# Taking 1/sum out of a DMA transpose and v out of a casting DMA, in a thresholded-attention and MLP kernel

## The chip, the cores and the metric

The kernel runs on one core of a Trainium2 chip, as one program from start to end. The metric is the device time of one execution in microseconds (us). A core has five engines with a queue each, worked off in order: PE (TensorE, matmuls; its weight loads are listed as PEld), DVE (VectorE), ACT (ScalarE), POOL (GpSimd) and SP (SyncE, which here only issues DMAs). They wait for each other through semaphores. PE writes to PSUM alone, eight banks of 2 KB in each of 128 partitions; ACT and DVE read PSUM; POOL works in SBUF.

## The reference

There are 8 batches, 8 heads, 576 tokens and 64 channels per head. After attention, the heads of a token are laid side by side (512 channels) and go through two linear layers.

```python
scores = scale * q @ k.T                        # per batch and head, 576 x 576
thresh = max(scores, -1) - tau                  # tau = 0.02
scores = where(scores >= thresh, scores, -1e9)
attn = exp(scores - max(scores, -1))
attn = attn / (sum(attn, -1) + 1e-9)
x = (attn @ v)                                  # tokens x 512 when the heads are joined
h = x @ w_in                                    # 512 -> 2048
out = maximum(0.01 * h, h) @ w_out              # 2048 -> 512
```

## The kernel before

The attention is cut into 72 **periods**, nine in each batch: for each half of the first 512 tokens (256 queries) four periods, one per pair of heads, and a ninth, the tail period, for the last 64 tokens of all heads. One period is four score tiles of 128 x 576: two query tiles `c` by two heads `h` of a pair. Period n of the main loop makes, in this order:

- PE: the scores (L223, 24 matmuls, each product as three fp16 halves); the turn of a q or k pair that a later period needs (L169, 16 small transposes into two PSUM banks, `tp`); then, in two halves, second-layer units (L369, two at a time, 8 matmuls), a first-layer unit (L356, 16 matmuls), again both; last the product of weights and v (L316, `pv`) of the period n - 2 (`PV_LAG`).
- DVE: four copies of score tiles out of PSUM, which also take the row minima (L256); 1/sum of the period before (L295) after the first copy; DVE's part of the turn's copy (L181, bank 1); the threshold (L267); three of the four weight tiles with their sums (L289); between the second and the third of these, `pv` times 1/sum into `x` (L336, in tail periods L328).
- ACT: its part of the turn's copy (L181 or L178, bank 0), the exponential of three tiles (L278), the leaky ReLU of each first-layer unit out of PSUM (`g`, L358), in every second period the copy of a finished 128 x 512 output (`osb`, L375), and the fourth tile's weights in two steps (L283, L284).
- POOL: splits one q or k pair into fp16 halves (L133, L140, L144) behind DVE's last weight tile of the period before, so that it runs beside the copies out of PSUM; between L133 and L140 it widens 1/sum to 64 columns per head as **a tenth block of the weights** (L299); it issues the loads of v and of the MLP's weights as DMAs that cast fp32 to fp16 (L92, L99, L103, L106).
- SP: turns the weights of the period before with one DMA transpose (L304: ten blocks of 128 for each c, fp16), then issues the period's loads of q and k, then stores.

PSUM has one tag `h` with two banks. A turn takes both, and then first-layer outputs `hp`, `pv` and the next turn take them in rotation, so the first `hp` of a period gets the bank that ACT's turn copy has emptied. In the first six periods (`early`), `pv` stands in front of the MLP's units, and 12 dummy matmul pairs (L481) fill PE in the first five. The order on each engine is the order in which the loop writes it; there is no scheduler.

Of the kernel before, what the change touches and what calls it, by code (L numbers as in the profile page):

```python
# [36 lines left out]
def kernel(  # L37
# [30 lines left out]

    raws, tails = {}, {}
    SRC = {"q": q, "k": k}  # L70
# [25 lines left out]
    def load_vtails(b):  # L96
        src = v[b, :, MAIN:S, :].rearrange("(r h) p d -> h p r d", h=2)
        for h in range(2):
            nc.gpsimd.dma_start(out=v16[b % 2][ds(64 * h, 64), :, 4 + h, :], in_=src[h])  # L99

# [21 lines left out]
    def new_half():  # L122
        return sb.tile([128, 2, 4, 2, 64], FP16, tag="half", bufs=6, name="half")

# [33 lines left out]
    def turn(keys, tags=("h", "h")):  # L158

        n = 2 if keys[0][1] == "t" else 4  # L160
        tp = [ps.tile([128, len(keys), 2, n, 64], FP16, tag=tag, bufs=2 if tag == "h" else 1, name="tp")
              for tag in tags]
        for i, key in enumerate(keys):
            half = halves.pop(key)
            for x in range(2):
                for t in range(n):
                    for r in range(2):
                        rows = ds(64 * r, 64)
                        nc.tensor.transpose(tp[r][:, i, x, t, :], half[rows, x, t, :, :].rearrange("p h d -> p (h d)"),  # L169
                                            ident[rows, rows])  # L170
            tps[key] = [t[:, i, :, :, :] for t in tp]

    def take(key, r, copy):
# [119 lines left out]
    def recip(st):  # L293
        rec = sb.tile([128, 2, 2], FP32, tag="rec", bufs=2, name="rec")
        nc.vector.reciprocal(out=rec[:, :, :], in_=st.sum[:, :, :])  # L295
        st.rec = rec

    def widen(st):
        nc.gpsimd.tensor_copy(out=st.w[:, :, 9, :].rearrange("q c (h d) -> q c h d", h=2),  # L299
                              in_=st.rec[:, :, :].unsqueeze(3).to_broadcast([128, 2, 2, 64]))  # L300

    def turn_w(st):
        st.wt = sb.tile([128, 2, 10, 128], FP16, tag="wT", bufs=4, name="wT")
        nc.sync.dma_start_transpose(out=st.wt[:, :, :, :].rearrange("k c n q -> k (c n) q"),  # L304
                                    in_=st.w[:, :, :, :].rearrange("q c n d -> q (c n d)"))

    def pv(st):
# [13 lines left out]
    def evacuate(st, ready):  # L321
        if st.tail:
            if st.b % 2 == 0:
                groups["t"] = xg = Group(128, (st.b, None))
                xg.x = sb.tile([128, NP, 128], FP16, tag="xt", bufs=2, name="xt")
            xg = groups["t"]
            o = xg.x[:, :, ds(64 * (st.b % 2), 64)]
            nc.vector.tensor_tensor(out=o, in0=st.pv[:, :, :].rearrange("d c (u q) -> d (c u) q", u=2),  # L328
                                    in1=st.wt[:, :, 9, :].rearrange("d c (u q) -> d c u q", u=2), op=AX.mult)
            done = st.b % 2 == 1  # L330
        else:
            if st.p == 0:
                groups["m"] = xg = Group(256, (st.b, 2 * st.blk))
                xg.x = sb.tile([128, NP, 256], FP16, tag="x", bufs=3, name="x")
            xg = groups["m"]
            nc.vector.tensor_tensor(out=xg.x[:, st.p, :].rearrange("d (c q) -> d c q", c=2), in0=st.pv[:, :, :],  # L336
                                    in1=st.wt[:, :, 9, :], op=AX.mult)
# [51 lines left out]

    loads_at, turns_at, split_at_, issue_at = {}, {}, {}, {}  # L390

    def at(d, n, f):
        d.setdefault(n, []).append(f)

    def split_pool(key, behind=None, between=lambda: None):
# [3 lines left out]
        between()  # L399
        split_high(key)  # L400
        split_low(key)
# [15 lines left out]
    for p in (2, 3):  # L417
        load_pair(p, "k", nc.sync)
        load_pair(p, "q", nc.sync)
    load_tails(0, "q")  # L420
    for t in v16:
# [18 lines left out]
    for i in range(4):  # L440
        load_w(i)
    for h in range(2):
        load_v(0, h)
    load_vtails(0)
    for key in ((0, 1, "k"), (0, 1, "q")):
# [8 lines left out]
    for key in ((0, 3, "k"), (0, 3, "q")):  # L454
        at(turns_at, 2, key)
    at(turns_at, 3, (0, "t", "q"))
    for i in range(4):
        at(issue_at, 5 + i, lambda i=i: load_w(4 + i))

    for b in range(1, B):  # L460
        base = PERB * (b - 1)
        for i, (s, w_) in enumerate(((0, "k"), (0, "q"), (1, "k"), (1, "q"))):
            at(loads_at, base + ((0, 1, 5, 6)[i] if b > 1 else (1, 2, 5, 6)[i]),
               lambda b=b, s=s, w_=w_: load_main(b, s, w_))
        for w_ in "kq":
            at(loads_at, base + (2 if b > 1 else 3), lambda b=b, w_=w_: load_tails(b, w_))
        order = [(0, "k"), (0, "q"), ("t", "k"), ("t", "q"), (1, "k"), (1, "q"), (2, "k"), (2, "q"), (3, "k"), (3, "q")]
        slots = (3, 4, 5, 5, 6, 7, 8, 9, 10, 11) if b > 1 else (4, 5, 7, 7, 6, 8, 9, 10, 11, 11)
        for n, (p, w_) in zip(slots, order):
            split_at(base + n, (b, p, w_))  # L470
        for h in range(2):
# [11 lines left out]

    def pv_of(n, ready):
        if n >= PV_LAG and n - PV_LAG < N:
            pv(periods[n - PV_LAG])
            return lambda: evacuate(periods[n - PV_LAG], ready)
        return lambda: None

    N = len(periods)  # L490
    n = 0
    while n < N + PV_LAG or l1q or l2q or stores:
        st = periods[n] if n < N else None
        before = periods[n - 1] if 1 <= n <= N else None
        early = n < 6
        keys = turns_at.get(n, [])
# [3 lines left out]
        if st:  # L500
            scores(st)
        if first_:
            turn(first_)
        if st:
# [4 lines left out]
        for i, key in enumerate(todo):  # L509
            if i == 0 and n > 2:  # L510
                split_pool(key, before.last, lambda: widen(before))
            else:
                split_pool(key)
# [12 lines left out]
        for f in issue_at.get(n, []):  # L526
            f()
        if st:
            exp_plain(st, 0)
        if early:  # L530
            if n < 5:
                idle(6)
            pv_of(n, n)()
            if n < 5:
                idle(6)
        for half in range(2):
            for _ in range(2):
                if l2q:
                    layer2()
            if l1q and l1q[0][3] <= n:  # L540
                layer1()
            if half == 0:
                for key in second:
                    turn([key])
            if st:
                if half == 0:
                    exp_plain(st, 1)
                    exp_plain(st, 2)
                    for key in second:
                        take(key, 0, on_act)  # L550
                else:
                    exp_steep(st, 3)
        x = (lambda: None) if early else pv_of(n, n + 1)
        if st:
# [3 lines left out]
        if st:  # L558
            weights(st, 1)
        x()  # L560
        if st:
# [35 lines left out]
```

## Time and profile before

| | |
|---|---|
| median of 3 runs | 522.95 us (522.0 to 527.2) |
| profiled execution | 523.43 us, of which the span is 521.6 us |
| PE, DVE, ACT, POOL busy | 88%, 85%, 77%, 44% of the span |
| DMA transposes of weights | 72, median 6.5 us from issue to landing |
| v loads through POOL | 16 of 256 KB (median 7.3 us), 16 of 32 KB (5.0 us) |

An entry such as `L256 DVE ... s<-sc` names the line of the kernel, the engine, and which tile is made from which. Times of single instructions overlap a little, since an engine starts one while the last of the former drains; the distance from start to start is what an engine can keep up. An idle time is put down to whatever ended last before the waiting instruction. "PEclk" is the clock that PE was granted, as a share of the full one.

### The profile page before, as it was taken

What the parts mean: (1) busy time and instruction counts of PE and PEld (TensorE: products, weight loads), DVE (VectorE), ACT (ScalarE), POOL (GpSimd) and SP (SyncE); (2) the same over time, 40 slices, a digit from 0 to 9 for tenths busy, and PEclk for the clock granted to TensorE, in tenths of its full rate; (3) what the DMA queues carried; (4) which work ended last, traced back from release to release, by engine and by line L of the source; (5) the groups of instructions that cost most, each with busy time, mean ns of one, the idle gap of its engine ahead of it and who ended that gap; (6) DMA issues with size and microseconds to landing.
All of it is one profiled execution on the core that took longest, in us unless ns stands there. A gap on an engine that the chain in (4) does not pass through costs nothing. (4 is left out here: it accounts for less than half of the span.)

```text
span 521.6 us, 19185 instructions
## 1 busy us (share of the span) xinstructions
PE 460.3 (88%) x7864; PEld 364.2 (70%) x7864; DVE 443.2 (85%) x1314; ACT 400.3 (77%) x704; POOL 228.2 (44%) x357
## 2 busy tenths in 40 slices
PE   3477674987989999989999999989999989999995
PEld 2455653665878777867788787877787868777773
DVE  3969693989999999999999999999999999999200
ACT  4737482778999988887879898879889987888541
POOL 5924372535554545454544555445545454000000
PEclk9969796999999999999999999999999999999999
DMA  8987999969989999989978999999998998656511
GB/s 211 178 183 125 159 170 142 202 122 169 192 160 201 146 213 166 183 165 174 205 154 192 139 223 165 201 149 209 153 212 160 178 176 167 133 103 153 133 43 60
DMA packets 230808, 85.65 MB, mean 164 GB/s; under 512 B 201024, under 2 KB 227648, under 8 KB 230720
## 3 DMA queue, kind: packets, MB, share of 16 engines
q1 hardware_dynamic: 214416, 75.12, 74.5%
q0 software_dynamic: 15488, 8.92, 14.0%
q8 instruction: 61, 1.00, 0.8%
q10 hardware_dynamic: 816, 0.39, 0.3%
q14 instruction: 27, 0.22, 0.1%
HBM read 36.70 MB, written 9.44 MB: 88 GB/s over the span
## 5 line engine op out<-in xcount | busy, mean ns | idle before, releaser
L256 DVE TENSOR_SCALAR_CACHE_REDUCE s<-sc 128x576 f32<-128x576 f32 x288 | 208.7, 745 | 5.2 <-PE sc L223 4.2
L289 DVE SCALAR_TENSOR_TENSOR w<-s,th,e 128x576 f16<-128x576 f32 x216 | 176.0, 840 | 9.0 <-ACT e L278 1.9
L278 ACT ACTIVATE e<-s,mn 128x576 f16<-128x576 f32 x216 | 158.7, 769 | 12.2 <-DVE s L256 12.0
L356 PEld LDWEIGHTS <-win 128*64 128x64 f16 x2560 | 134.5, 111 | 32.6 <-issue 9.3
L369 PE MATMUL o<-wout,g 128*64 128x512 f16 x1152 | 150.3, 383 | 0.7 <-ACT osb L375 0.7
L356 PE MATMUL hp<-x,win 128*64 128x256 f16 x2048 | 135.8, 275 | 5.9 <-ACT qT L181 2.6
L223 PE MATMUL sc<-kT,qT 64*128 64x384 f16 (+7 forms) x1920 | 124.3, 292 | 8.7 <-DVE qT L181 6.8
L358 ACT ACTIVATE g<-hp 128x512 f16<-128x512 f32 x144 | 85.4, 593 | 45.4 <-PE hp L356 44.2
L223 PEld LDWEIGHTS <-qT 64*128 64x128 f16 (+1 forms) x1920 | 94.3, 99 | 31.2 <-issue 13.0
L133 POOL TENSOR_SCALAR scaled<-raw 128x512 f32<-128x512 f32 x60 | 37.6, 627 | 161.7 <-DVE w L289 114.8
L369 PEld LDWEIGHTS <-g 128*64 128x64 f16 x1152 | 62.0, 110 | 35.3 <-issue 3.5
L144 POOL TENSOR_TENSOR half<-scaled,half 128x512 f16<-128x512 f32 (+1 forms) x75 | 80.9, 1079 | 6.4
L316 PE MATMUL pv<-wT,v 128*64 128x256 f16 (+1 forms) x960 | 54.5, 252 | 28.8 <-DMA wT<-w 28.8
L316 PEld LDWEIGHTS <-v 128*64 128x64 f16 x960 | 41.2, 112 | 33.7 <-DMA wT<-w 29.7
L284 ACT ACTIVATE w<-s,minus_tau 128x576 f16<-128x576 f32 x72 | 55.8, 775 | 6.0 <-issue 0.4
L283 ACT ACTIVATE s<-s,th 128x576 f32<-128x576 f32 x72 | 55.7, 773 | 0.8 <-DVE th L267 0.7
L299 POOL CAST w<-rec 128x256 f16<-128x256 f32 x72 | 29.2, 405 | 57.6 <-DVE rec L295 53.1
L169 PE MATMUL tp<-ident,half 64*128 64x64 f16 x1152 | 33.4, 194 | 12.5 <-ACT half L154 6.8
L140 POOL CAST half<-scaled 128x512 f16<-128x512 f32 (+1 forms) x75 | 43.5, 580 | 0.8
L169 PEld LDWEIGHTS <-half 64*128 64x128 f16 x1152 | 30.2, 97 | 19.1 <-issue 9.6
L336 DVE TENSOR_TENSOR x<-pv,wT 128x256 f16<-128x256 f32 x64 | 26.9, 421 | 19.3 <-PE pv L316 19.2
L181 ACT COPY kT<-tp 128x512 f16<-128x512 f16 x32 | 18.6, 580 | 21.8 <-PE tp L169 21.3
(39 smaller groups left out, 248.5 us busy)
## 6 DMA issues: line engine op xcount, KB each, us to landing
out_dram<-osb SPq DMA_DIRECT2D x16, 512.0 KB, 6.0
raw<-in_k_dram SPq DMA_DIRECT2D x14, 512.0 KB, 4.9
raw<-in_q_dram SPq DMA_DIRECT2D x14, 512.0 KB, 5.1
v<-in_v_dram POOLq DMA_DIRECT2D x16, 256.0 KB, 7.3
win<-in_moe_w_in_dram POOLq DMA_DIRECT2D x4, 512.0 KB, 8.5
wout<-in_moe_w_out_dram POOLq DMA_DIRECT2D x4, 512.0 KB, 11.4
wT<-w SPq DMA_TRANSPOSE x72, 6.5
raw<-in_k_dram SPq DMA_DIRECT2D x4, 256.0 KB, 5.9
```

The costliest lines, as they stand in the source:

```text
L144: nc.gpsimd.tensor_tensor(out=halves[key][:, 1, 0:n, :, :], in0=scaled.pop(key)[:, 0:n, :, :], in1=halves[key][:, 0, 0:n, :, :], op=AX.sub ...
L169: nc.tensor.transpose(tp[r][:, i, x, t, :], half[rows, x, t, :, :].rearrange("p h d -> p (h d)"), ident[rows, rows])
L223: yield nc.tensor.matmul(out=o, lhsT=lhs, rhs=turned[st.b, "k"][rows, kx, pair, ds(key0, n)], start=(i == 0), stop=(i == 2), skip_group_ch ...
L256: return nc.vector.tensor_scalar(out=st.s[TILES[n]][:, :], in0=sc[:, ds(PLACE[TILES[n]], 576)], scalar1=-1.0 / UNIT, scalar2=None, op0=AX. ...
L278: nc.scalar.activation(out=st.e[t][:, :], in_=st.s[t][:, :], func=AF.Exp, bias=st.mn[:, n : n + 1], scale=-1.0)
L283: nc.scalar.activation(out=z, in_=z, func=AF.Prelu, bias=st.th[:, n : n + 1], scale=-1.0, alpha=1e20)
L284: nc.scalar.activation(out=w_of(st, t), in_=z, func=AF.Exp, bias=minus_tau[:, :], scale=1.0, accum_out=st.sum[:, c, h : h + 1])
L289: st.last = nc.vector.scalar_tensor_tensor(out=w_of(st, t), in0=st.s[t][:, :], scalar=st.th[:, n : n + 1], in1=st.e[t][:, :], op0=AX.is_le ...
L316: nc.tensor.matmul(out=o, lhsT=v16[st.b % 2][:, 2 * c + u if st.tail else st.p, blk, :], rhs=rhs, start=(i == 0), stop=(i == 4), skip_grou ...
L356: nc.tensor.matmul(out=hp[ds(64 * c, 64), jj, :], lhsT=w_in16[:, i, ds(128 * j + 64 * c, 64)], rhs=g.x[:, i, :], start=(i == 0), stop=(i = ...
L358: nc.scalar.activation(out=g.g[:, ds(nj * u, nj), :], in_=hp[:, :, :], func=AF.Prelu, bias=0.0, scale=1.0, alpha=0.01)
L369: nc.tensor.matmul(out=g.o[ds(64 * c, 64), :], lhsT=g.g[:, j, ds(128 * m + 64 * c, 64)], rhs=w_out16[:, j, :], start=(j == 0), stop=(j == ...
```

## The change

1/sum is no longer part of the tile that the DMA turns: `w` and `wT` have nine blocks for each c instead of ten, and the widening on POOL goes. DVE writes 1/sum as fp16. PE spreads and turns it: four transposes for the period n - 2 (two query tiles, two heads; a column of 1/sum, read 64 times over, against the identity), right behind the scores and the first turn of period n, into the unused upper half of the bank that the turn takes first; without a turn it takes a bank of tag `h` of its own. ACT copies the 128 x 256 result out (`by`) behind its turn copies, and DVE's product reads `by`.

v is loaded as fp32 by SP, four heads at a time (512 KB, two loads in a batch, and two for the tail), into staging tiles, and cast to fp16 by POOL: two copies of 128 x 256 per pair of heads, at the end of POOL's work in four of nine periods, the tail's two copies in the last of these; batch 0's first pair and tail by ACT in period 0. One of six staging tiles for halves goes. For the periods 2 to 4, `pv` moves from the front to the end of the period, as in the later ones; the dummy matmuls stand in one run.

```diff
-        st.w = sb.tile([128, 2, 10, 128], FP16, tag="w", bufs=3, name="w")
+        st.w = sb.tile([128, 2, 9, 128], FP16, tag="w", bufs=3, name="w")
...
     def recip(st):
-        rec = sb.tile([128, 2, 2], FP32, tag="rec", bufs=2, name="rec")
-        nc.vector.reciprocal(out=rec[:, :, :], in_=st.sum[:, :, :])
-        st.rec = rec
-
-    def widen(st):
-        nc.gpsimd.tensor_copy(out=st.w[:, :, 9, :].rearrange("q c (h d) -> q c h d", h=2),
-                              in_=st.rec[:, :, :].unsqueeze(3).to_broadcast([128, 2, 2, 64]))
+        st.rec = sb.tile([128, 2, 2], FP16, tag="rec", bufs=4, name="rec")
+        with nc.allow_low_precision(reason="as the weights"):
+            nc.vector.reciprocal(out=st.rec[:, :, :], in_=st.sum[:, :, :])
...
+    def spread(st, bank):
+        bank = bank or ps.tile([128, 1024], FP16, tag="h", bufs=2, name="tp")
+        for c in range(2):
+            for h in range(2):
+                nc.tensor.transpose(bank[ds(64 * h, 64), ds(512 + 128 * c, 128)],
+                                    st.rec[:, c, ds(h, 1)].to_broadcast([128, 64]), ident[:, :])
+        return bank
+
+    def take_spread(st, bank):
+        st.by = sb.tile([128, 2, 128], FP16, tag="by", bufs=2, name="by")
+        nc.scalar.copy(out=st.by[:, :, :], in_=bank[:, 512:768].rearrange("d (c q) -> d c q", c=2))
...
-    def load_v(b, h):
-        nc.gpsimd.dma_start(
-            out=v16[b % 2][:, :, ds(6 * h, 4), :].rearrange("p r t d -> p r (t d)"),
-            in_=v[b, :, 0:MAIN, :].rearrange("(r h) (p t) d -> h p r (t d)", h=2, t=4)[h])
+    def load_v(b, s):
+        t = sb.tile([128, 4, 256], FP32, tag="vraw", bufs=2, name="vraw")
+        nc.sync.dma_start(out=t[:, :, :], in_=v[b, ds(4 * s, 4), 0:MAIN, :].rearrange("h (p t) d -> p h (t d)", t=4))
+        vraws[b, s] = t
...
+    def cast_v(b, p, copy=None):
+        copy = copy or nc.gpsimd.tensor_copy
+        src = vraws[b, p // 2][:, ds(2 * (p % 2), 2), :].rearrange("p h (t d) -> p h t d", d=64)
+        dst = v16[b % 2][:, p, :, :].rearrange("p (h t) d -> p h t d", h=2)
+        for h in range(2):
+            copy(out=dst[:, h, ds(h, 4), :], in_=src[:, h, :, :])
...
-        if first_:
-            turn(first_)
+        bank = turn(first_) if first_ else None
+        due = periods[n - PV_LAG] if PV_LAG <= n < N + PV_LAG else None
+        if due:
+            bank = spread(due, bank)
...
         if before:
-            if not todo or n <= 2:
-                widen(before)
             turn_w(before)
+        for f in pool_at.get(n, []):
+            f()
...
+        if due:
+            take_spread(due, bank)
         if st:
             exp_plain(st, 0)
...
-        for h in range(2):
-            at(issue_at, base + 4 + 3 * h, lambda b=b, h=h: load_v(b, h))
-        at(issue_at, base + 8, lambda b=b: load_vtails(b))
+        for s in range(2):
+            at(loads_at, base + 4 + 3 * s, lambda b=b, s=s: load_v(b, s))
+        at(loads_at, base + 8, lambda b=b: load_vtails(b))
+        for p in range(NP):
+            at(pool_at, base + (6, 7, 9, 10)[p], lambda b=b, p=p: cast_v(b, p))
+        at(pool_at, base + 10, lambda b=b: cast_vtails(b))
```

More of the change, by code (lines that the diff above doesn't have):

```diff
@@ L89, in load_tails, with cast_vtails @@
         tails[b, which] = t
-    def load_v(b, h):
-        nc.gpsimd.dma_start(
-            out=v16[b % 2][:, :, ds(6 * h, 4), :].rearrange("p r t d -> p r (t d)"),
-            in_=v[b, :, 0:MAIN, :].rearrange("(r h) (p t) d -> h p r (t d)", h=2, t=4)[h])
+    def load_v(b, s):
+        t = sb.tile([128, 4, 256], FP32, tag="vraw", bufs=2, name="vraw")
+        nc.sync.dma_start(out=t[:, :, :], in_=v[b, ds(4 * s, 4), 0:MAIN, :].rearrange("h (p t) d -> p h (t d)", t=4))
+        vraws[b, s] = t
     def load_vtails(b):
+        t = sb.tile([128, NP, 64], FP32, tag="vrawt", bufs=1, name="vrawt")
         src = v[b, :, MAIN:S, :].rearrange("(r h) p d -> h p r d", h=2)
         for h in range(2):
-            nc.gpsimd.dma_start(out=v16[b % 2][ds(64 * h, 64), :, 4 + h, :], in_=src[h])
+            nc.sync.dma_start(out=t[ds(64 * h, 64), :, :], in_=src[h])
+        vtails[b] = t
+    def cast_v(b, p, copy=None):
[4 more added lines that the diff above has]
+            copy(out=dst[:, h, ds(h, 4), :], in_=src[:, h, :, :])
+    def cast_vtails(b, copy=None):
+        copy = copy or nc.gpsimd.tensor_copy
+        t = vtails.pop(b)
+        for h in range(2):
+            copy(out=v16[b % 2][ds(64 * h, 64), :, 4 + h, :], in_=t[ds(64 * h, 64), :, :])
     def load_w(i):
@@ L122, in new_half @@
     def new_half():
-        return sb.tile([128, 2, 4, 2, 64], FP16, tag="half", bufs=6, name="half")
+        return sb.tile([128, 2, 4, 2, 64], FP16, tag="half", bufs=5, name="half")
     def split_scale(key):
@@ L160, in turn @@
         n = 2 if keys[0][1] == "t" else 4
-        tp = [ps.tile([128, len(keys), 2, n, 64], FP16, tag=tag, bufs=2 if tag == "h" else 1, name="tp")
-              for tag in tags]
+        banks = [ps.tile([128, 1024], FP16, tag=tag, bufs=2 if tag == "h" else 1, name="tp") for tag in tags]
+        tp = [t[:, 0 : 128 * n * len(keys)].rearrange("d (i x t p) -> d i x t p", x=2, t=n, p=64) for t in banks]
         for i, key in enumerate(keys):
@@ L171, in turn @@
             tps[key] = [t[:, i, :, :, :] for t in tp]
+        return banks[0]
     def take(key, r, copy):
@@ L387, in store, with split_pool @@
                 nc.sync.dma_start(out=out[ds((b + u) * S + MAIN, 64), :], in_=g.osb[ds(64 * u, 64), 0, :])
-    loads_at, turns_at, split_at_, issue_at = {}, {}, {}, {}
+    loads_at, turns_at, split_at_, pool_at, act_at = {}, {}, {}, {}, {}
     def at(d, n, f):
         d.setdefault(n, []).append(f)
-    def split_pool(key, behind=None, between=lambda: None):
+    def split_pool(key, behind=None):
         mm = split_scale(key)
@@ L398, in split_pool @@
             tc.add_manual_dep(mm.ins, behind.ins.name, BEHIND, reason="beside VectorE's reads of PSUM")
-        between()
         split_high(key)
@@ L419 @@
         load_pair(p, "q", nc.sync)
+    for s in range(2):
+        load_v(0, s)
+        if s == 0:
+            load_vtails(0)
     load_tails(0, "q")
@@ L456 @@
     at(turns_at, 3, (0, "t", "q"))
+    at(act_at, 0, lambda: cast_v(0, 0, on_act))
+    at(act_at, 0, lambda: cast_vtails(0, on_act))
+    for p in range(1, NP):
+        at(pool_at, 2, lambda p=p: cast_v(0, p))
     for i in range(4):
-        at(issue_at, 5 + i, lambda i=i: load_w(4 + i))
+        at(pool_at, 5 + i, lambda i=i: load_w(4 + i))
     for b in range(1, B):
@@ L482, in idle @@
                                  start=True, stop=True, skip_group_check=True)
[L484 to L488, printed above, removed]
     N = len(periods)
@@ L494 @@
         before = periods[n - 1] if 1 <= n <= N else None
-        early = n < 6
+        early = n == 5
         keys = turns_at.get(n, [])
@@ L509 @@
         for i, key in enumerate(todo):
[L510 to L513, printed above, removed]
+            split_pool(key, before.last if i == 0 and n > 2 else None)
         if before:
-            if not todo or n <= 2:
-                widen(before)
             turn_w(before)
+        for f in pool_at.get(n, []):
+            f()
         for f in loads_at.get(n, []):
@@ L525 @@
                 widen_keys(key[0])
-        for f in issue_at.get(n, []):
-            f()
+        if due:
+            take_spread(due, bank)
         if st:
             exp_plain(st, 0)
+        if n < 5:
+            idle(12)
         if early:
[L531 to L535, printed above, removed]
+            pv(due)
+            evacuate(due, n)
         for half in range(2):
@@ L541 @@
                 layer1()
+            if half == 1 and due and not early:
+                pv(due)
             if half == 0:
@@ L550 @@
                         take(key, 0, on_act)
+                    for f in act_at.get(n, []):
+                        f()
                 else:
                     exp_steep(st, 3)
-        x = (lambda: None) if early else pv_of(n, n + 1)
         if st:
@@ L559 @@
             weights(st, 1)
-        x()
+        if due and not early:
+            evacuate(due, n + 1)
         if st:
```

13 lines of the change are left out of this document (6 added, 7 removed).

## The prediction

> **What bounds the kernel now.** I read first the table of busy time by stretch, cut where DVE's first score copy of periods 0, 3, 12, 63 starts and after the last product `pv` x 1/sum but one. Columns: stretch, its length, busy time of PE, PEld, DVE, ACT, POOL, granted clock, DMA share, GB/s.
>
> ```profile
> 12.96:39.50 26.54, 15.96 (x253) 13.20 (x251) 21.44 (x55) 14.41 (x24) 16.10 (x20) 0.83 0.96 178
> 39.50:110.71 71.21, 49.55 (x804) 39.63 (x802) 56.13 (x165) 44.67 (x77) 33.69 (x51) 0.87 1.01 158
> 110.71:432.27 321.56, 306.09 (x5424) 243.78 (x5421) 308.29 (x925) 277.57 (x490) 162.77 (x253) 1.00 0.98 177
> 432.27:482.70 50.43, 50.43 (x813) 39.41 (x810) 49.09 (x150) 43.42 (x75) 8.28 (x15) 1.00 0.65 136
> ```
>
> The early stretches have idle engines; the third (51 periods of 6.31 us) has PE at 95% and DVE at 96%, with the DMA engines full. Two engines share the bound there, so the next views are who waits, and then one period by itself. Of the waits, these name what the change is about (total us, times, longest), and the timeline of DVE shows where they are large:
>
> ```profile
> PE pv L316 <- DMA wT<-w: 28.8, 15, 7.8
> DVE x L336 <- PE pv L316: 19.2, 11, 7.0
> ```
>
> ```profile
> 34.57 0.42 DVE L336 TENSOR_TENSOR x<-pv,wT 128x256 f16<-128x256 f32 x1 [2.24 <-PE pv L316]
> ...
> 56.85 0.43 DVE L336 TENSOR_TENSOR x<-pv,wT 128x256 f16<-128x256 f32 x1 [2.37 <-PE pv L316]
> 59.94 0.82 DVE L289 SCALAR_TENSOR_TENSOR w<-s,th,e 128x576 f16<-128x576 f32 x1 [1.93 <-ACT e L278]
> ...
> 86.91 0.42 DVE L336 TENSOR_TENSOR x<-pv,wT 128x256 f16<-128x256 f32 x1 [7.04 <-PE pv L316]
> ```
>
> Three stalls in periods 2, 5 and 8 hold most of it; in the 51 periods of the third stretch DVE waits for `pv` 4.6 us in all. What paces those is seen in the timeline around the first `hp` of period 64, a period after one with an `osb` copy:
>
> ```profile
> 442.45 0.58 ACT L375 ACTIVATE osb<-o 128x512 f32<-128x512 f32 x1
> ...
> 442.93 0.59 ACT L358 ACTIVATE g<-hp 128x512 f16<-128x512 f32 x1
> ...
> 443.41 0.78 ACT L283 ACTIVATE s<-s,th 128x576 f32<-128x576 f32 x1
> ...
> 444.27 0.78 ACT L284 ACTIVATE w<-s,minus_tau 128x576 f16<-128x576 f32 x1
> 444.37 0.40 PE L169 MATMUL tp<-ident,half 64*128 64x64 f16 x16
> ...
> 444.69 1.05 PE L369 MATMUL o<-wout,g 128*64 128x512 f16 x8
> ...
> 445.04 0.56 ACT L181 COPY qT<-tp 128x512 f16<-128x512 f16 x1
> ...
> 445.51 0.78 ACT L278 ACTIVATE e<-s,mn 128x576 f16<-128x576 f32 x1
> 445.66 0.60 PE L356 MATMUL hp<-x,win 128*64 128x256 f16 x7
> ```
>
> PE could start `hp` at 445.58 (the two `o` units take 0.89 from start to start), but ACT, late from `osb`, frees the bank at 445.60: `hp` starts at 445.66, 6.11 after the one before (439.55). Without `osb` it is PE alone, 433.60 to 439.55, 5.95. The pair makes 6.03 a period; DVE's own pace is 6.05 (438.32 to 444.38). **PE, ACT and DVE are tied**, so work added to PE or to ACT ahead of `hp` lengthens the period, and work taken from POOL or DMA shortens only stalls.
>
> **The change, part by part.** The sum is made against the profiled execution, 523.4 us (span 521.6), 0.5 above the median.
>
> *Early DMA waits.* The transpose of period 6 is issued at 69.79 and lands 15.8 us later, while a q load, two `w_out` loads and v share the DMA engines; the median is 6.5. After the change it carries nine tenths of the blocks, is issued when the weights are done and not 0.8 to 1.3 us later behind POOL's widening, and v's casting load is out of its way; `w_out` and the q load stay. I let it land 7 us sooner: of the 7.04 + 1.20 us of DVE's idle time in period 8, 6 go (between 3, if `w_out` alone makes it late, and 8). In period 5 the transpose took 8.3 us beside v; at the median it lands about when PE gets there, so of 2.37 + 1.93 + 0.46, 4 go (2 to 4.7). In period 2 `pv` moves to the period's end: 2.24, and the 1.18 us for the next scores, go: 3 (2 to 4). Periods 9 to 11 have another 1.5 us of waits; the spread and the casts there cost about as much: 0.
>
> *The start.* The price of the three is at ACT in period 0: it now casts v's tail, and behind that cast stand ACT's weights of period 0, whose sum DVE needs for 1/sum of period 0 at 21.25. v's loads are queued on SP behind q and k and are in flight with `w_in`, whose four loads are issued by 10.87 and the last of which lands 11.8 us later, at 22.6. The same small tail loads as q has, undisturbed, land in 3.0 us; v's tail on POOL's queue, behind `w_in`, landed at 25.8. Ends: no wait, or DVE held until 28. The nearest row to judge by is a load beside a casting one: q at 66.56 with `w_out` at 66.04 landed at 75.42 and 75.19, together, 8.9 us against a median of 5.1. So I take v's tail to land with `w_in`, at 23, DVE to go on at 25.5, 4 us late. It gets back 1.5 in period 1, where POOL's splits (done by then) held up DVE's weights (1.73 instead of 0.81 at 24.43). Net of period 2's gain: 0 (-5 to +3).
>
> On that row, the Trainium skill (DMA: Bandwidth & Descriptors, Queues, rings and completion order) says that a DMA engine goes round-robin between queues by whole packets. The trace agrees: the two loads ended 0.23 us apart; by the rule the start costs what I took, by the 3.0 us row nothing.
>
> *Spread on PE.* Four transposes in each period, 512 columns in all against 1024 of a turn, which takes 0.33 from start to next start; `pv`, in the same halves of the array, takes 0.64 for 2560. That gives 0.13 to 0.16; ends 0.05 and 0.33. I take 0.13. In the 9 periods without turns and the two behind them PE has no gap at all (50.43 busy of 50.43), so it counts there in full: **+1.4**.
>
> *Copy on ACT, and what waits for it.* A copy of 128x256 out of PSUM takes 0.37 (L178). It stands between the turn's copy and the exponential, and `hp` needs its bank. In the program as built, ACT's first turn copy also waits until the spread is done, since both share a bank. After an `osb`: the turn copy at 445.04, the next start 0.47 later, plus 0.37, bank free 0.28 later than now: 6.11 becomes 6.39. Otherwise: turn at 432.38, copy at 432.81, now 0.13 later, then 0.47 + 0.37 + 0.06 to `hp`: 1.46 after the turn's start instead of 1.22 (433.60): 5.95 becomes 6.19. Mean 6.29, **0.24 above DVE's 6.05**: in 51 periods +12.2. Bounds: 0 where ACT's idle time before `g` (0.6, PE's `hp`) hides all, 0.48 if the two copies don't overlap (0.37 + 0.06 whole in both kinds).
>
> *What that replaces.* 51 x 6.05 = 308.6 of 321.6: 13.0 us are stalls today: waits for `pv` and what follows them, and DVE held by POOL (the threshold once took 1.18 instead of 0.17 beside L144 at 224.38, weights 1.13 in six periods beside the tail's splits). All but some 2 fall under the slower pace or vanish. The loss and the gain cancel: **+1** (-11 to +14).
>
> *Casts on POOL.* 0.40 each (L140, 128x256); widening (0.40) goes. Two more in three of nine periods, after which POOL ends at about the threshold; in the fourth, the batch's last split plus four casts, it ends some 4 us after the copies begin (0.63 + 0.62 + 1.17 and 4 x 0.40), and the threshold and first weights, 3.2 and 3.5 after, wait: at most 0.9 (the 1.73 row), 0.5 taken, seven times. DVE then has 0.24 a period to spare, and I count it in the 2 above; without that cover, 3.5.
>
> Beside the 1.73 row, the Trainium skill (SBUF — State Buffer, Who interferes with whom) has DVE with two SBUF inputs and a POOL read exclude each other for a whole instruction. The trace agrees (+0.91 beside L144); by it a cast costs at most its own 0.40, so the two instructions that wait lose 0.8 at most, and the sum would be 2 us higher by that end.
>
> *SP.* Four more issues a batch; each load (0.58) stands behind the period's transpose (3.1 to 3.6), in a period of 6.
>
> Sum: -4 (period 5) - 6 (period 8) + 0 + 1 + 1.4 = -7.6: **516**, from 511 to 521 by its own terms.
>
> **The rivals.**
>
> 1. *The copy hides.* ACT idles 44 us before `g`; if the bank is free in time, DVE keeps 6.05 and the 13 us are gained but for 2: 516 - 12 = 504 to 506. Against: `hp` already waits for ACT after every `osb`. 13%.
> 2. *ACT becomes PE's clock, at the higher price.* Place: between the turn's first copy and the first `hp`. At 0.48 a period it costs 24.5, 12.3 more than forecast: **528**, slower; from 0.38 on the change gains nothing. For: the bank is shared and the wait for the spread is in it; against: ACT overlaps copies today (0.47 start to start). 20%.
> 3. *The transposes stay late* (the change doesn't do what it says): v now stands in SP's queue ahead of the next transpose, 512 KB at a time in four of nine periods with q or k loads or stores; period 8 and 5 keep their stalls. 516 + 10 = 526. For: DMA share 0.98 all along; against: a tenth of the largest traffic (74.5% on SP's queue) goes. 22%.
>
> The forecast has 45%. About 1% (5 us) is what a measurement of this kernel can tell from no change. Faster by more (below 517.7): two thirds of the forecast's 45 and all of rival 1: 0.42. Slower by more (above 528.2): half of rival 2 and a little of 3, and what I don't see, mostly at the start: 0.26. Range 505 to 529.
>
> **What would show it.** In the profile after: the waits of `pv` for the transpose under 8 us; DVE's idle time before `x` in periods 5 and 8 under 2; `hp` waiting for ACT's `by` copy in most periods, with 6.2 to 6.4 us from `hp` to `hp`, and DVE busy share in the middle falling to about 94%; a wait of ACT for v's tail in period 0 of about 4. If `hp` starts on time, rival 1; if DVE's waits for `pv` stay, rival 3. A start that loses over 5 us makes all of it too low.

## The result, and the profile after

The changed kernel takes **542.46 us** (median of 4 runs, 541.0 to 544.6) against 522.55 in the same comparison (522.0 to 527.2): a ratio of 1.036, 95% interval 1.029 to 1.044. It is slower by 3.6%, 26 us above the forecast and outside its range. The profiled execution took 543.29 us, its span is 541.4.

The table of busy time by stretch, cut where DVE's first score copy of periods 0, 3, 12, 63 and 71 starts (columns as before: stretch, length, PE, PEld, DVE, ACT, POOL, granted clock, DMA share, GB/s):

```profile
14.96:36.84 21.88, 14.90 (x258) 12.52 (x256) 20.30 (x56) 15.78 (x29) 14.53 (x20) 0.84 1.06 198
36.84:108.36 71.52, 48.72 (x840) 38.95 (x837) 56.21 (x164) 46.63 (x86) 34.34 (x49) 0.93 1.07 159
108.36:448.51 340.15, 315.27 (x5628) 251.05 (x5625) 316.66 (x924) 287.62 (x539) 146.75 (x232) 1.00 0.78 168
448.51:497.86 49.35, 48.02 (x795) 37.69 (x790) 47.06 (x140) 43.12 (x80) 6.86 (x12) 1.00 0.60 125
```

The third row holds the loss. The same 51 periods took 321.56 us and now take 340.15: 6.67 a period instead of 6.31. The DMA engines are no longer full there (share 0.78 instead of 0.98), and yet PE (93%) and DVE (93%) both have gaps. The waits say which (total us, times, longest):

```profile
DVE x L361 <- PE pv L341: 17.6, 49, 6.1
PE hp L381 <- DVE qT L197: 14.0, 25, 1.9
PE hp L381 <- DVE kT L197: 12.8, 26, 2.1
...
PE pv L341 <- DMA wT<-w: 10.1, 2, 7.1
```

The last line is what the change was to improve, and it did: 28.8 us in 15 waits are now 10.1 in 2, both before period 10. In the middle the transposes land 3.0 to 6.4 us ahead of `pv`. But two lines are new. PE's `hp` waits 51 times for **DVE's** copy of the turn (`qT`, `kT`), and 49 times DVE's `x` waits for PE's `pv` (11 times before, in the prediction's lines). One period around such a wait, from the timeline:

```profile
267.81 0.76 DVE L272 TENSOR_SCALAR_CACHE_REDUCE s<-sc 128x576 f32<-128x576 f32 x1
...
268.25 0.30 PE L324 MATMUL tp<-ident,rec 128*64 128x128 f16 x4
...
268.50 0.17 DVE L312 RECIPROCAL rec<-sum 128x4 f16<-128x4 f32 x1
268.58 0.73 DVE L272 TENSOR_SCALAR_CACHE_REDUCE s<-sc 128x576 f32<-128x576 f32 x1
268.60 0.58 ACT L197 COPY qT<-tp 128x512 f16<-128x512 f16 x1 [0.36 <-PE tp L324]
269.08 0.38 ACT L330 COPY by<-tp 128x256 f16<-128x256 f16 x1
...
269.24 0.42 DVE L197 COPY qT<-tp 128x512 f16<-128x512 f16 x1
...
269.71 1.06 PE L381 MATMUL hp<-x,win 128*64 128x256 f16 x16 [0.29 <-DVE qT L197]
...
273.09 0.42 DVE L361 TENSOR_TENSOR x<-pv,by 128x256 f16<-128x256 f32 x1 [0.17 <-PE pv L341]
...
273.44 0.81 DVE L305 SCALAR_TENSOR_TENSOR w<-s,th,e 128x576 f16<-128x576 f32 x1
...
274.35 0.76 DVE L272 TENSOR_SCALAR_CACHE_REDUCE s<-sc 128x576 f32<-128x576 f32 x1
...
275.30 0.18 DVE L312 RECIPROCAL rec<-sum 128x4 f16<-128x4 f32 x1 [0.18 <-ACT w L300]
...
276.52 1.06 PE L381 MATMUL hp<-x,win 128*64 128x256 f16 x16 [0.56 <-DVE kT L197]
```

ACT's two copies, the one the forecast was worried about among them, end at 269.46, ahead of DVE's at 269.66, and it is the latter that releases `hp`. The program as built says the same: the first `hp` of a period now waits for DVE's turn copy, the second for ACT's `by`. In the kernel before, the first took the bank that ACT empties, and the largest of its few waits was for ACT's copy:

```profile
PE hp L356 <- ACT qT L181: 2.6, 3, 1.0
```

**The two banks of tag `h` have changed places.** DVE empties its bank only after two score copies and 1/sum. That closes a loop between PE and DVE. From start to start it is 3.38 from `hp` to `x`, 0.35 to the last weights, 0.91 to the next score copy and 1.90 to the next `hp`, in all 6.54; where 1/sum has to wait for ACT's late sum the last leg takes 2.17, and the loop 6.81. The mean of the two kinds is 6.67, as long as the mean period.

The second loss is early. DVE's idle times before `x` in periods 8 and 9:

```profile
77.94 0.42 DVE L361 TENSOR_TENSOR x<-pv,by 128x256 f16<-128x256 f32 x1 [2.73 <-PE pv L341]
...
91.45 0.42 DVE L361 TENSOR_TENSOR x<-pv,by 128x256 f16<-128x256 f32 x1 [6.10 <-PE pv L341]
```

The stall that was one of 7.04 us is now two, of 2.73 and 6.10: the transposes of periods 6 and 7 still take 13.2 and 19.8 us.

The runs of two kernels below (e1 and e3) fell into two groups some 10 us apart, about the length of these early stalls, which e1's profiled execution (in its lower group) does not have and e3's (in its upper group) has; so e1 has no interval, e3's rests on the lower group, and for these two the pace of the profiled execution says more than the median.

### The profile page after: what moved, and what is told of

It reads as the page before. It is cut to its first block, busy times and chain, and to the rows that moved or that the text cites. A ratio compares the mean times of both kernels' runs of the same rounds, so it can differ in the third digit from the quotient of the medians.

```text
span 541.4 us, 19764 instructions
## 1 busy us (share of the span) xinstructions
PE 469.5 (87%) x8152; PEld 372.8 (69%) x8152; DVE 452.6 (84%) x1314; ACT 417.5 (77%) x780; POOL 209.3 (39%) x329
## 3 DMA queue, kind: packets, MB, share of 16 engines
HBM read 36.70 MB, written 9.44 MB: 85 GB/s over the span
## 4 chain that ended last, share of the span: by engine, by line
PE 52%; DVE 20%; ACT 16%; issue 6%; DMA 5%; ACTq 0%; DVEq 0%
PE hp L381 23%; PE o L394 13%; DVE s L272 10%; PE sc L239 9%; PE pv L341 6%; ACT w L300 5%; ACT g L383 4%; DMA wT<-w 4%; ACT s L299 4%; DVE w L305 3%; ACT e L294 2%; DVE kT L197 2%; DVE qT L197 2%; DVE rec L312 1%; DMA rawt<-in_k_dram 1%
## 5 line engine op out<-in xcount | busy, mean ns | idle before, releaser
L381 PEld LDWEIGHTS <-win 128*64 128x64 f16 x2560 | 132.9, 110 | 66.1 <-issue 41.3
L381 PE MATMUL hp<-x,win 128*64 128x256 f16 x2048 | 135.1, 273 | 29.4 <-DVE qT L197 14.0
L394 PE MATMUL o<-wout,g 128*64 128x512 f16 x1152 | 148.7, 379 | 0.7 <-ACT osb L400 0.7
L394 PEld LDWEIGHTS <-g 128*64 128x64 f16 x1152 | 66.5, 110 | 28.2 <-issue 1.0
L341 PE MATMUL pv<-wT,v 128*64 128x256 f16 (+1 forms) x960 | 54.3, 249 | 13.6 <-DMA wT<-w 10.1
L341 PEld LDWEIGHTS <-v 128*64 128x64 f16 x960 | 42.8, 111 | 15.3 <-DMA wT<-w 10.8
L361 DVE TENSOR_TENSOR x<-pv,by 128x256 f16<-128x256 f32 x64 | 27.1, 423 | 20.3 <-PE pv L341 17.6
L184 PE MATMUL tp<-ident,half 64*128 64x64 f16 x1152 | 32.0, 193 | 12.4 <-ACT half L169 8.8
L197 ACT COPY qT<-tp 128x512 f16<-128x512 f16 x32 | 18.4, 576 | 14.7 <-PE tp L324 13.9
```

Source lines behind the costliest of these rows:

```text
L341: nc.tensor.matmul(out=o, lhsT=v16[st.b % 2][:, 2 * c + u if st.tail else st.p, blk, :], rhs=rhs, start=(i == 0), stop=(i == 4), skip_grou ...
L381: nc.tensor.matmul(out=hp[ds(64 * c, 64), jj, :], lhsT=w_in16[:, i, ds(128 * j + 64 * c, 64)], rhs=g.x[:, i, :], start=(i == 0), stop=(i = ...
L394: nc.tensor.matmul(out=g.o[ds(64 * c, 64), :], lhsT=g.g[:, j, ds(128 * m + 64 * c, 64)], rhs=w_out16[:, j, :], start=(j == 0), stop=(j == ...
```

## The experiments

Theory A: the swapped banks cost the middle. Theory B, the forecast's second rival: ACT's copy and PE's transposes, as work, cost it. Theory C: v's loads on SP and its casts on POOL cost it. For the stalls in periods 8 and 9, the question is whether `w_out`'s casting loads or the loads of q, k and v make the transposes late. "Pace" is the mean period from period 12 to 63, "`hp` idle" PE's idle time in front of `hp` with `x`, both from the profiled execution. The kernel before was run again beside each group, with medians from 524.0 to 527.1.

| kernel | median us (lowest to highest) | ratio to before, 95% interval | pace us | `hp` idle us |
|---|---|---|---|---|
| before | 522.55 (522.0 to 527.2) | | 6.305 | 5.9 |
| after | 542.46 (541.0 to 544.6) | 1.036 (1.029 to 1.044) | 6.670 | 29.4 |
| e1 other bank | 525.26 (516.2 to 526.4) | none | 6.388 | 15.8 |
| e2 other bank, late copy | 512.71 (511.9 to 513.5) | 0.975 (0.967 to 0.982) | 6.103 | 8.3 |
| e3 DVE's turn copy first | 507.49 (501.7 to 514.7) | 0.955 (0.945 to 0.965) | 6.137 | 6.8 |
| e8 `by` copied twice | 541.20 (539.7 to 542.1) | 1.029 (1.022 to 1.036) | 6.670 | 29.4 |
| e4 1/sum alone | 540.40 (539.9 to 541.1) | 1.029 (1.019 to 1.038) | 6.669 | 28.3 |
| e5 v alone | 516.73 (512.7 to 520.8) | 0.981 (0.970 to 0.992) | 6.186 | 7.3 |
| e6 `w_out` early | 546.04 (541.1 to 549.5) | 1.036 (1.024 to 1.049) | 6.670 | 27.7 |
| e7 e2 and `w_out` early | 507.03 (503.9 to 509.0) | 0.965 (0.956 to 0.974) | 6.103 | 6.3 |
| e10 e2 without `w_out` | 502.34 (501.7 to 503.0) | 0.958 (0.953 to 0.963) | 6.104 | 8.0 |
| e9 e2 and `w_out` spread out | **499.42** (498.2 to 500.4) | 0.953 (0.947 to 0.959) | 6.103 | 7.1 |
| e11 e2, `w_out` not cast | 499.16 (498.7 to 501.2) | 0.953 (0.947 to 0.958) | 6.103 | 7.4 |
| e12 before, `w_out` spread out | 524.01 (519.8 to 526.2) | 0.999 (0.995 to 1.002) | 6.345 | 5.8 |

### e1: 1/sum into the other bank

```diff
     def turn(keys, tags=("h", "h")):
...
-        return banks[0]
+        return banks[1]
```

> Theory A (banks swapped): in the changed kernel the first hp of a period gets the bank that DVE empties behind two score copies, so PE waits for DVE and DVE in turn for PE, 6.67 us a period in the middle. Here 1/sum is spread into the bank that DVE empties, and the program as built gives the first hp ACT's bank again; nothing else moves. A: first hp no longer waits for DVE's turn copy; ACT's copy by now waits for DVE's turn copy and holds the exponentials some 0.5 us, so 6.1 to 6.3 us a period, 512 to 525. Theory B (ACT's added copy and PE's added transposes are what PE lost time to, the second rival of the forecast): both are still there, so 6.6 or more a period, 536 to 545.

The pace falls to 6.39 and the median to 525.3, both just above what A gave and well below what B gave. No `hp` with `x` waits for DVE's turn copy any more, while ACT's copy `by` now waits for it, as A said, 56 times and more than was expected:

```profile
ACT by L330 <- DVE kT L197: 22.9, 29, 1.5
ACT by L330 <- DVE qT L197: 22.2, 27, 1.5
```

ACT stands still 0.8 us each time, ahead of the exponential, and the next turn copy is late from it: `hp` now waits for ACT (6.9 us for `qT`, 4.6 for `kT`). So a cure of the banks alone makes a new wait, and ACT's place in the order does matter once the banks are right.

### e2: the same, and ACT's copy behind the first exponential

```diff
-        return banks[0]
+        return banks[1]
...
-        if due:
-            take_spread(due, bank)
         if st:
             exp_plain(st, 0)
+        if due:
+            take_spread(due, bank)
```

> As the former kernel, and ACT's copy by moved behind the first exponential, so that it no longer waits for DVE's turn copy. A: 6.05 to 6.15 us a period in the middle (DVE's own pace, and 0.05 to 0.1 for ACT), 509 to 515. B: the same work on ACT and PE, 536 to 545.

6.103 a period and 512.7 us: A, and below the kernel before by 2.5%, with all the added work of the change still on PE, ACT and POOL. The timeline of one period shows the order that A wants:

```profile
255.67 0.75 DVE L272 TENSOR_SCALAR_CACHE_REDUCE s<-sc 128x576 f32<-128x576 f32 x1
...
256.98 1.04 PE L381 MATMUL hp<-x,win 128*64 128x256 f16 x16
...
257.09 0.42 DVE L197 COPY qT<-tp 128x512 f16<-128x512 f16 x1
...
257.54 0.37 ACT L330 COPY by<-tp 128x256 f16<-128x256 f16 x1 [0.20 <-DVE qT L197]
```

`hp` starts 1.31 us after the first score copy, with no idle time in front of it, and before DVE has begun its turn copy; in the changed kernel it started 1.90 after, behind that copy. DVE's next first score copy starts at 261.73, 6.06 later, with no wait in between: DVE sets the pace, at what the forecast took for its own (6.05).

### e3: DVE's turn copy ahead of its second score copy

```diff
         if before:
             recip(before)
-        copy_min(st, 1)
         taken()
+        copy_min(st, 1)
         copy_min(st, 2)
```

> The changed kernel with DVE's turn copy ahead of its second score copy; the first hp still gets DVE's bank. A: hp starts 0.7 us sooner in its period, so PE and DVE no longer hold each other; some 6.1 to 6.2 us a period, 512 to 520. B: DVE does the same work and ACT's copy stands where it stood, at most 0.25 a period less, 530 or more.

The banks stay swapped here; only DVE empties its own sooner. Pace 6.137, as A said, and PE's idle time before `hp` is down to 6.8 us. No bank, no work and no copy of ACT moved, and the loss went all the same. So B falls by a second, independent edit. The median is below A's range, the profiled execution (514.7) in it.

### e8: ACT's copy made twice

```diff
-        nc.scalar.copy(out=st.by[:, :, :], in_=bank[:, 512:768].rearrange("d (c q) -> d c q", c=2))
+        for _ in range(2):
+            nc.scalar.copy(out=st.by[:, :, :], in_=bank[:, 512:768].rearrange("d (c q) -> d c q", c=2))
```

> The changed kernel with ACT's copy by made twice, some 0.28 us more of ACT in each of 72 periods. A: ACT's copy is not on the path of the first hp, whose bank DVE gives, so 541 to 549 (only hp's second bank and the exponentials come later). B: if ACT's copy sets PE's pace, its whole 0.28 counts in 51 or more periods, 556 to 562.

541.2, and the pace is the changed kernel's to the third digit. The pair of copies takes 0.78 in place of 0.38, and the waits of `hp` are what they were:

```profile
PE hp L382 <- DVE qT L197: 14.0, 25, 1.9
PE hp L382 <- DVE kT L197: 12.8, 26, 2.1
```

Twice the work in this copy costs nothing: as the changed kernel stands, ACT's copy is not on the path. (Once the banks are right it is: between e1 and e2 it moves, and the pace with it by 0.29.)

### e4 and e5: each half of the change by itself

e4 (the first diff, its tail loads only) takes v back to POOL's casting loads, and keeps 1/sum on TensorE; e5 (the second) takes 1/sum back into the tenth block and POOL's widening, and keeps v as fp32.

```diff
-            nc.sync.dma_start(out=t[ds(64 * h, 64), :, :], in_=src[h])
+            nc.gpsimd.dma_start(out=v16[b % 2][ds(64 * h, 64), :, 4 + h, :], in_=src[h])
```

```diff
-        st.w = sb.tile([128, 2, 9, 128], FP16, tag="w", bufs=3, name="w")
+        st.w = sb.tile([128, 2, 10, 128], FP16, tag="w", bufs=3, name="w")
...
+    def widen(st):
+        nc.gpsimd.tensor_copy(out=st.w[:, :, 9, :].rearrange("q c (h d) -> q c h d", h=2),
+                              in_=st.rec[:, :, :].unsqueeze(3).to_broadcast([128, 2, 2, 64]))
```

> The changed kernel with v back on POOL's casting DMA: 1/sum by TensorE alone. Theory A (the swapped banks, which come with the spread): the middle stays at 6.6 to 6.7 us a period, 537 to 546. Theory C (v's loads in SP's queue and the casts on POOL cost the time): 6.3 or less a period, 515 to 528.

> The changed kernel with 1/sum again as a tenth block, widened by POOL and turned by DMA: v as fp32 alone. A: no spread, no swap of banks, 6.2 to 6.35 us a period in the middle, 515 to 524. C: 6.6 or more, 537 to 546.

Both came out as A said (e5's pace a hair under its range). With 1/sum alone the pace is 6.669: the whole loss of the middle comes with the spread. With v alone it is 6.186, better than before by 0.12 a period, and the kernel is faster by 1.9%. C falls: v's loads and casts cost the middle nothing. Not all of the 1.9% is theirs, since e5 keeps the later `pv` of the periods 2 to 4, too: its period 2 takes 6.68 instead of 10.56.

### e6 and e7: `w_out` in earlier periods

```diff
-        at(pool_at, 5 + i, lambda i=i: load_w(4 + i))
+        at(pool_at, 1 + i, lambda i=i: load_w(4 + i))
```

e6 is the changed kernel with this edit, e7 has it with e2's.

> The changed kernel with the four casting loads of w_out issued in periods 1 to 4 instead of 5 to 8. If these loads are what still holds the transposes of periods 6 and 7 (13 and 20 us to land), the stalls of 2.7 and 6.1 us before x in periods 8 and 9 go and most of the 10 us: 532 to 537, with perhaps 1 to 2 us of new waits in periods 2 to 5. If q, k and v loads hold them: 541 to 544, stalls as before.

> Both mends: 1/sum into DVE's bank with ACT's copy behind the first exponential, and w_out issued in periods 1 to 4. If the two causes are apart and add: 502 to 508, below the kernel before by 14 us or more. If the early stalls only move elsewhere: 509 to 515.

e6 met neither expectation. In periods 6 to 9 the transposes land in 4.6 to 4.7 us and DVE does not wait: where the loads of `w_out` are gone, so is the stall. But the transposes of periods 2 and 3 now take 15.3 and 15.7 us, DVE waits 5.18 and 3.96 before `x` in periods 4 and 5, and the time is not lower. The stall went where the loads went. e7, at 507.0, is in its range, since e2's pace is in it; it has the moved stall, too (5.72 and 1.43).

### e9, e10, e11: what it is about these loads

All three have e2's banks and late copy. e10 does not load `w_out` and sets it to zero; e9 loads it in every other period; e11 reads the same bytes by SP in fp32 into a staging tile, and uses zeros (a tile a quarter as large, not among the lines below). The output of e10 and e11 is therefore zero. The diffs, in the order e9, e10, e11:

```diff
-        at(pool_at, 5 + i, lambda i=i: load_w(4 + i))
+        at(pool_at, 1 + 2 * i, lambda i=i: load_w(4 + i))
```

```diff
+        at(pool_at, (1, 3, 4, 5)[i], lambda i=i: nc.gpsimd.memset(w_out16[:, ds(4 * i, 4), :], 0.0))
```

```diff
+        t = sb.tile([128, 2, 512], FP32, tag="wraw", bufs=3, name="wraw")
+        nc.sync.dma_start(out=t[:, :, :], in_=moe_w_out[ds(256 * i, 256), :].rearrange("(j p) f -> p j f", p=128))
...
+        for h in range(2):
+            at(loads_at, 5 + i, lambda i=i, h=h: load_raw(2 * i + h))
```

> 1/sum in DVE's bank with ACT's copy behind the first exponential (512.7 before), and the second layer's weights not loaded at all: they are set to zero on chip, so the output is zero and this part of the work is left out. If the four casting loads make the transposes of periods 6 and 7 late (14.5 and 21.1 us): they land in 5 to 7 us, DVE does not wait in periods 8 and 9, and the time is 499 to 503. If q, k and v loads do it alone: 510 to 514.

> The same with the loads of w_out kept, one in each of periods 1, 3, 5, 7 instead of 5 to 8. If what makes the transposes late is that each load is still in flight when the next is issued: no transpose over 10 us, 500 to 505. If the 2 MB on top of full DMA engines cost their time wherever they stand: the same 10 to 13 us of DVE's waiting, in other periods, 509 to 514.

> The same 2 MB read in periods 5 to 8, but by SP, in fp32 without a cast, into a staging tile that nothing reads (the second layer's weights are zeros, so the output is zero). If the casting loads on POOL's queue are what holds up the transposes: these land in 10 us at most and the time is 499 to 504. If the bytes read are: late transposes and a stall of 8 us or more as before, 508 to 514.

e10: without the loads none of the first ten transposes takes over 6.4 us and DVE's waits of periods 8 and 9 are gone; 502.3, 10.4 below e2 (the kernel before took 524.0 beside e10 and 527.0 beside e2). (Its zeros cost something themselves: POOL's memsets of 1.80 us stand beside DVE in periods 1, 3, 4 and 5, and period 3 takes 7.07 in place of 5.91.) e9: the loads are all there, each landed before the next is issued; the first ten transposes take 10.4 us at most, and DVE waits for none of them: 499.4, just below the range that went with it. So it is not that the bytes are too many. The ranges of e9, e10 and e11 (498.2 to 503.0) lie well below e2's (511.9 to 513.5). e11: the same bytes in the same periods as in e2, read in fp32 by SP, do next to no harm: no transpose over 9.4 us, 499.2. The DMA issues of the stretch, first of the changed kernel (57 to 95 us), then of e11 (50 to 83); the columns are engine, count, size of one, and median us to landing:

```profile
wout<-in_moe_w_out_dram POOLq DMA_DIRECT2D x3, 512.0 KB, 11.9
...
wT<-w SPq DMA_TRANSPOSE x5, 8.8
```

```profile
wraw<-in_moe_w_out_dram SPq DMA_DIRECT2D x8, 512.0 KB, 4.9
...
wT<-w SPq DMA_TRANSPOSE x6, 6.6
```

The size of a casting load is what it writes; it reads twice that, so both kernels read 4 MB of `w_out` (the 2 MB of the two expectations are what the cast leaves of them). In the changed kernel a casting load that takes 12 us is still in flight when the next period issues another, and every transpose between them is late. Overlap of the loads is not enough by itself, though: in e1's profiled execution two of them are in flight, too, when the next is issued, by 1 to 2 us, and the transposes land in 9.6 and 9.9 us.

### e12: the kernel before, with `w_out` spread out

```diff
-        at(issue_at, 5 + i, lambda i=i: load_w(4 + i))
+        at(issue_at, 1 + 2 * i, lambda i=i: load_w(4 + i))
```

> The kernel before, with its w_out loads in periods 1, 3, 5, 7 instead of 5 to 8. If these loads alone made the transposes of periods 6 and 7 late (15.8 and 17.2 us), also with v and the tenth block in the DMAs: the 8.2 us of idle time in period 8 go, 512 to 517. If the tenth block and v's casting loads were the cause, as the forecast had it: the transposes stay over 10 us, 520 to 527.

The transposes of periods 6 and 7 come down to 8.6 and 9.3 us, with the tenth block and v's casting loads still there, and the idle time of period 8 is gone. The total did not move. Of the 8.4 us won in period 8, 3.3 were lost in period 2, 1.4 in period 4 and 1.9 in period 9; another 2.0 came in the middle, which this edit does not touch. Period 2 shows why loads in early periods cost this kernel time:

```profile
37.59 0.42 DVE L336 TENSOR_TENSOR x<-pv,wT 128x256 f16<-128x256 f32 x1 [5.52 <-PE pv L316]
```

In this kernel `pv` stands in front of the MLP's units in periods 2 to 5, so the transpose of period 0, with a `w_out` load now beside it (9.3 us instead of 6.9), holds up the whole of period 2: 7.4 us of idle time in DVE instead of 4.1. The change moved the `pv` of the periods 2 to 4 to the end, and e9 has the same early loads without that wait.

## Why the prediction was wrong

Its table of costs against the span (521.6 to 541.4, +19.8), by the starts of DVE's first score copies:

| part | forecast us | measured us |
|---|---|---|
| to period 3 | 0 | -2.66 |
| periods 3 to 5 | -4 | -3.20 |
| periods 6 to 9 | -6 | +4.21 |
| periods 10 and 11 | 0 | -0.70 |
| the 51 periods of the middle | +1 | +18.59 |
| period 63 to the end | +1.4 | +3.56 |

**The step that failed** is "*Copy on ACT, and what waits for it*", in the words "and `hp` needs its bank". I took it that the first `hp` still gets ACT's bank, since it had before, and priced ACT's delay: 6.29 a period. The bank was DVE's. ACT's copy was priced at 0.24 a period, and in the changed kernel a second one adds nothing (e8). The wait for DVE's turn copy, which I had nowhere, is worth 0.53 to 0.57 a period (6.670 against 6.137 in e3, where only that copy moved, and 6.103 in e2). The built program shows which release each `hp` waits for; I read there that ACT's turn copy waits for the spread, but not this. I carried the rotation of the banks over from the kernel before as I had described it there, and this is where the loss lies.

The other half of that sum, "13.0 us are stalls today" that "fall under the slower pace or vanish", was right: with the banks put right, the middle takes 311.26 us (e2) instead of 321.56, and 10.3 of the 13.0 are gone. Rival 1 ("the copy hides", DVE keeps its 6.05) is nearly what e2 does (6.10), not the kernel forecast; rival 2 had the right sign, the right place (between the turn and the first `hp`) and the wrong engine. Rival 3 was half right: the transposes did stay late in periods 6 and 7, though not because v stands in SP's queue.

**Period 8** failed, too, by 10 us. I let the transpose land 7 us sooner because it carries a tenth less and v's casting load is out of its way, with `w_out` named as the lower end. It took 2.6 less, and the next one 2.6 more (13.2 and 19.8 us against 15.8 and 17.2). The tenth block and v's casting load did not decide: with both in place, spreading `w_out` brought the two transposes to 9 us (e12), and with `w_out`'s casting loads spread out, gone or replaced by SP's the stall is gone (e9, e10, e11). With the loads where they were it need not come (e1). So these loads are needed for it, and what else it takes stays open.

**Periods 2 and 5** were right: period 2 went from 10.56 to 6.83 us (3.7 gained, 3 forecast), period 5 from 10.88 to 7.33 (3.6 gained, 4 forecast). In period 2 it is the moved `pv`, since e4 and e5 have it alike (6.84 and 6.68). In period 5 the transpose came down from 8.3 to 4.8 us as forecast; which half of the change does how much of it stays open (8.30 in e4, 9.00 in e5, but 8.06 and 8.88 in e1 and e3 as well).

**The start** came out within its bounds by luck. ACT did not wait for v's tail. I had it in flight with `w_in` and landing at 23; v's loads were issued ahead of `w_in` (8.14 to 10.30 against 10.98) and the tail landed at 14.6. On the rule of the Trainium skill (DMA: Bandwidth & Descriptors, Queues, rings and completion order) that I leaned on there, that a DMA engine takes turns between queues packet by packet, the changed kernel's tail says nothing; in e5 a v load issued at 9.44, inside `w_in`'s (8.89 to 10.71), landed at 24.74 beside their last at 24.56, as the rule has it: from 13 to 22 us the DMA engines took 433 packets from POOL's queue (1.58 MB) and 422 from SP's (0.43 MB), so that SP's queue, with the smaller packets, moved about a quarter as many bytes. The first period starts 2.0 us later than before, but the profiled executions have that start anywhere from 12.9 to 15.0, with v on SP at both ends (e5 at 12.87, the changed kernel at 14.96).

**The spread** was right in size: 0.14 from start to next start (268.25 to 268.39). The five periods from 66 to 70 grew by 0.10 on average, 0.5 in all. The last row of the table has more in it: 1.8 of it are the periods 63 to 65, where the pace of the middle goes on, and 1.2 the end of the span, where DVE's last two products wait 2.70 and 4.12 us instead of 1.97 and 3.86.

**The casts on POOL** were put at 3.5 without cover and 0 with it: e4, without them, has the same pace as the changed kernel (6.669 and 6.670), and with DVE as the bound (e2) two thresholds in the middle took 0.39 instead of 0.17 and five weight tiles 0.94 to 0.95 instead of 0.81, beside the casts of v's tail: some 1.1 us in all. The Trainium skill's rule on DVE and POOL (SBUF — State Buffer, Who interferes with whom) would have allowed 0.8 for each of seven; the runs show less. What it can explain went the other way: six weight tiles of 1.12 beside the tail's splits, in the kernel before and in e5, are gone in the changed kernel and in e2 (none over 0.95).

Of the signs that the forecast named: waits of `pv` for the transpose under 8 us, it was 10.1; DVE's idle before `x` in period 5 none, in period 8 2.73 and in period 9 6.10; `hp` waiting for `by` did not come, and the pace of 6.2 to 6.4 was 6.67; DVE's share of the middle fell to 93% as named, but by another wait.

## What to carry to other kernels

When a change puts a new writer or reader on a rotating buffer, look up in the built program which release each later user waits for: here four small transposes swapped two banks, and the wait that came from it cost 27 us in the middle by e3 and 29 by e2, where the work itself cost next to nothing. A bank should be handed to the first user by the engine that empties it first; where that can't be chosen, move the emptying copy forward in its engine's order (e3). Before crediting a lighter DMA with a stall's end, take away the other transfers of that stretch one at a time; and spread casting loads so that each lands before the next is issued, which ended the stall here (e9), if nothing else waits for the transposes that then run beside them (e12).

## What the runs showed of the hardware

- A casting load of 512 KB on POOL's queue next to DMA transposes takes 9.6 to 17.1 us in the changed kernel (57 to 95 us), and the transposes between two of them 13 to 21 (changed kernel and e2). In its stretches of 5 us from 70 to 90 us the changed kernel moves 86 to 180 GB/s with the DMA engines shown as busy throughout (a share of 1.09 to 1.57; 86 GB/s at 1.46, from 85 to 90 us). The same reads on SP's queue without a cast, half as large each, land in 4.2 to 5.8 us, the transposes in 9.4 at most, at 241 to 293 GB/s with a share of 0.97 to 1.15 (e11, 50 to 80 us). Busy DMA engines are not a measure of what they move. Whether the cast or the queue does it, e11 does not tell apart: it changed both.
- In the profiled execution of e1 the same late transposes came only to 9.6 and 9.9 us, at 198 to 242 GB/s between 65 and 80 us, and periods 8 and 9 had no stall, with the loads where they are in e2 (14.5 and 21.1). So the slow-down is not fixed by where the loads stand; what sets it off stays open.
- Where POOL's and SP's queues both had work, the DMA engines took as many packets from each, not as many bytes: 433 and 422 packets, 1.58 and 0.43 MB (e5, 13 to 22 us).
- Which bank the pool hands out first: in the changed kernel, e1 and e2 alike, the first `hp` got the bank that the spread was not put into. Why stays open.
